# Batch 0's block means of v by products with its own tiles, and the dense layer's first chunk in two runs of pieces

## The chip, the cores and the metric

One core of a Trainium2 chip runs the kernel; the other cores are idle. The metric is the device time of one execution in microseconds; lower is better. The engines are named as in the profile: PE (TensorE) multiplies, PEld is its weight load, DVE (VectorE), ACT (ScalarE) and POOL (GpSimd) work on elements, and SP (SyncE) here only issues DMAs, in the order in which they stand in its program.

## What is computed

```python
# attention: q, k, v are (2, 8, 768, 64); window 16, block 32
k_sum = k.reshape(B, H, nb, block, D).max(axis=3)
v_sum = v.reshape(B, H, nb, block, D).mean(axis=3)      # the block means of v
scores_l = where(|i - j| < 16, scale * q @ k.T, -1e9)
scores_s = scale * q @ k_sum.T + log(block)
a = softmax(concat([scores_l, scores_s]))
x = (a @ concat([v, v_sum])).reshape(1536, 512)
...
# dense layer, 512 -> 2048 -> 512
h = x @ w_in
g = where(h > 0, h, exp(min(h, 0)) - 1)
x = g @ w_out
...
# router and experts: top 1 of 8 by cosine, then relu(x @ w1[e]) @ w2[e] times the gate
```

The weights of the dense layer arrive as 64-bit floats (the kernel reads them as pairs of 32-bit words).

## The kernel before

**Attention.** Each batch has 8 heads, taken as 4 pairs. A pair has 12 query tiles of 64 tokens, in 3 groups of four, so a batch has 12 groups, numbered `sc0` to `sc11` and so on. For a pair the tile `vw` holds, for each query tile, 96 rows of v around it (loaded by `load_v`, `vw<-in_v_dram`, two loads of the middle and four of the ends) and in rows 96 to 119 the 24 block means. `kw` holds keys and block maxima (`ks`) alike, `qbd` the queries. A group runs scores (`sc`, PE), mask with row minimum (`pt`, `mn`, DVE, L395), exp (ACT, L400), sums' reciprocal (DVE), scaling (POOL, L413), transposes (`tp`, PE), their copy (`pT`), products with `vw` (`pv`, PE), and a split of the result into a high and a low part (`xT`, ACT L448 and DVE L456).

The block means come from a second load of v: `load_vst` (L205) brings four heads with a block to each partition, as 96 rows of 32 x 64. `v_summary` sums the first four heads on DVE (four reductions, L213), `v_summary_pool` the other four on POOL (nine additions, L227); `load_vsum` sends the mean tile `vm` by DMA into rows 96 to 119 of `vw`, repeated for the 12 query tiles.

**Dense layer.** The 768 tokens of a batch are two chunks of 384. The 2048 hidden columns are 16 pieces of 128. A step is one piece for one chunk, 64 steps in all: batch 0 chunk 0 with pieces 0 to 15, then chunk 1, then batch 1's chunks. A piece's weights are loaded as pairs of words (`rw`, `rv`), scaled on ACT or POOL (L156, L154) and put together by three DVE operations for each half (L170, L172, L176, `cv` and `vt`); both chunks and both batches use the result `vt`. In each step they are split into a high part (ACT, L186) and a low part (DVE or POOL, L190), both in `wt`. Then come twelve `hp` products (L557 to L559), ELU on ACT and DVE (`e`, `gt`, L564 to L581), and nine `y` products (L596 to L598) that add up over a chunk's 16 steps in three PSUM banks. `y_out` copies these (ACT, L605) and stores them.

**Order.** A string, `ORDER`, lists the program by hand as atoms: `sc3` is the scores of group 3, `b4.00` a conversion of piece 4, `up5` the `hp` products of step 5, `dn5` its `y` products, a letter after a colon the engine. In before it covers batch 0's attention and the steps up to 11 (`G0 = 12`). From there a loop writes each step, and batch 1's attention is put between steps 12 and 37 by `at_step` and `attn_slots`. Each engine runs its share in that order; waits are on tiles and buffers. SP issues a load only when the eighth load before it is in.

Of the kernel before, what the change touches and what calls it, by code (L numbers as in the profile page):

```python
# [41 lines left out]
C_N = C_SLOT + NSLOT  # L42
# [9 lines left out]
lk00:l lk01 c0 lk10:s lk11 lk20:l lq00 lq01 lq20 c1 lt0 ox1 kt00 kt01 mq0 mq1 km00:v km01:v ks0 ke01:a ke00:v  # L52
mk0 kt11 qt00 qo001:a qo000:a qt01 qo011:a qo010:a le01 lk21 lq21 kt10 km10:a lq30 lk30:l le00 kw0:p km11:v
ox0 sc0 sc2 ks1 ex0 ex2 vs00 sc1 ke10:v ex1 kw1:a rt0 no0:p mk1 lq10 ke11:p rt2 no2:p kt20 lq11 qt10 qt11
qo110:a lk31 lv00 lq31 vs01 vs02 qo101:v qo100:v qo111:a vs03 rt1 no1:p kt31 qt20 kt21 km20:a km21:a tr0 sc3
lt1 lv01 le11 td0:a ls01 ls00 ke20:v ex3 ks2 kw2:a vs10 vs11 vs12 ke21:p tr2 sc4 ex4 qo200:v sc5 qt30 lv10
# [25 lines left out]
def fused_kernel(ctx, tc, q, k, v, w_in, w_out, emb, tau, w1, w2, consts, toks, minit, out):  # L82
# [137 lines left out]
    def v_summary_pool(b, r, n0, n1):  # L220
# [7 lines left out]
        if n1 == 10:  # L228
            vsum[b, r] = vm = at.tile([4 * NBLK, D], F32, tag="vm", name="vm", bufs=3)
# [4 lines left out]
    QK = {}  # L234
# [229 lines left out]
    def attn_slots(b):  # L464

        NG, LAG = 3 * NPAIR, 3
        normed = [0]

        def drain(d):

            if d < 2:
                a_out(b, NG - 5 + d)
            if d < 3:
                a_tr(b, NG - 3 + d)
                a_turned(b, NG - 3 + d)
                a_pv(b, NG - 4 + d)
            if d == 2:
                a_out(b, NG - 3)
            if d == 3:
                a_out(b, NG - 2)  # L480
                a_pv(b, NG - 1)
            if d == 4:
                a_out(b, NG - 1)

        def slot(s):
            p, r = s // 3 + 1, s % 3
            prep = s < NG and p < NPAIR
            if s >= NG:
                drain(s - NG)
                return  # L490
            if prep and r == 0 and s:
                prep_k(b, p)
                prep_k_out(b, p)
            if 0 <= s - LAG - 2 < NG:
                a_out_hi(b, s - LAG - 2)
            if s < NG:
                a_scores(b, s)
                a_exp(b, s)
            if s == 0:
                prep_k(b, p)  # L500
                prep_k_out(b, p)
            if s == 1:
                prep_ks(b, p)
            if prep and r:
                prep_q(b, p, r - 1)
            if prep and r == 1:
                prep_w(b, p)
            while normed[0] < (s - 1 if s < NG - 3 else s if s < NG - 1 else NG):
                a_root(b, normed[0])
                a_norm(b, normed[0])  # L510
                normed[0] += 1
            if prep and r:
                prep_q_out(b, p, r - 1)
            if 0 <= s - LAG - 2 < NG:
                a_out_lo(b, s - LAG - 2)
            if 0 <= s - LAG < NG:
                a_tr(b, s - LAG)
                a_turned(b, s - LAG)
            if prep and r == 0 and s:
                prep_ks(b, p)  # L520
            if 0 <= s - LAG - 1 < NG:
                a_pv(b, s - LAG - 1)
            if prep and r == 0 and p + 2 < NPAIR:
                load_k(b, p + 2)
            if prep and r == 2 and p + 2 < NPAIR:
                load_q(b, p + 2)
# [774 lines left out]
```

## Time and profile before

| | us |
|---|---|
| runs of the kernel, median of 3 | 562.68 (561.32 to 563.0) |
| the profiled execution, its own time | 561.42 |
| its span in the trace | 559.6 |
| PE, DVE, ACT, POOL busy | 517.4, 425.7, 354.0, 270.7 |
| first dense step starts | 55.76 |
| step 32 (batch 1) starts | 229.67 |

The span is the time from the first to the last instruction of one execution; the own time holds also what lies around it. Busy time counts an engine's instructions as the profiler saw them; an engine's idle time costs something only where the others wait for it. PE's matmul records come two to a product where the operands are 32-bit floats, so counts in the trace are larger than in the program.

### The profile page before, as it was taken

How to read it: one execution, taken by the hardware profiler on the slowest of the kernel's cores; microseconds unless marked ns; L12 is line 12 of the kernel's file. 1: busy time of each engine (PE TensorE's matmuls, PEld its weight loads, DVE VectorE, ACT ScalarE, POOL GpSimd, SP SyncE). 2: the span in 40 equal slices, each digit the busy share in tenths (PEclk: the TensorE clock that was granted, in tenths of full speed). 3: DMA queues.
4: the chain of work that ended last, by engine and by line, in shares of the span. 5: the costliest groups of instructions: out<-in, count | busy, mean ns of one | idle time of the engine just before them, and what ended most of it. 6: DMA issues, size and time to landing. Idle time of an engine off the chain costs nothing.

```text
span 559.6 us, 10282 instructions
## 1 busy us (share of the span) xinstructions
PE 517.4 (92%) x3270; PEld 455.2 (81%) x3270; DVE 425.7 (76%) x1053; ACT 354.0 (63%) x870; POOL 270.7 (48%) x274
## 2 busy tenths in 40 slices
PE   4986898999899999998999999999999999999991
PEld 4765786879788898896888998889779989999980
DVE  4999999988997665488776488866899777656671
ACT  3888685666767675565476655665565586566570
POOL 1477686876385332344457546765376532121010
PEclk9999998999999999999999999999999999999997
DMA  8999865669302014020100223718946399965000
GB/s 216 205 262 218 301 216 201 177 168 218 108 1 53 20 35 169 20 77 19 37 2 2 75 57 95 249 54 281 340 163 208 111 339 316 335 215 181 20 29 14
DMA packets 98939, 81.28 MB, mean 145 GB/s; under 512 B 38159, under 2 KB 83599, under 8 KB 98368
## 3 DMA queue, kind: packets, MB, share of 16 engines
q1 hardware_dynamic: 96256, 73.72, 44.7%
q0 software_dynamic: 2624, 6.84, 3.4%
q8 instruction: 28, 0.46, 0.4%
q14 instruction: 31, 0.25, 0.2%
HBM read 73.03 MB, written 6.94 MB: 143 GB/s over the span
## 4 chain that ended last, share of the span: by engine, by line
PE 31%; issue 8%; DVE 7%; ACT 5%; POOL 3%; POOLq 0%; ACTq 0%; DVEq 0%
PE shp L891 3%; PE o L914 3%; PE shp L892 3%; PE shp L890 3%; PE o L915 3%; PE o L913 3%; DVE ydj L640 3%; POOL wt L190 2%; DVE e L573 2%; PE y L598 1%; ACT wt L186 1%; DVE wt L190 1%; PE y L596 1%; PE y L597 1%; ACT gt L577 1%
## 5 line engine op out<-in xcount | busy, mean ns | idle before, releaser
L581 POOL TENSOR_TENSOR gt<-e,gt 128x384 fp32r<-128x384 f32 x63 | 64.0, 1016 | 87.7 <-ACT gt L577 50.1
L190 POOL TENSOR_TENSOR wt<-vt,wt 128x512 fp32r<-128x512 f32 x60 | 79.5, 1333 | 39.4 <-ACT wt L186 35.1
L190 DVE TENSOR_TENSOR wt<-mv,wt 128x512 fp32r<-128x512 f32 x113 | 80.6, 750 | 15.3 <-ACT wt L186 8.2
L557 PE MATMUL hp<-xT,wt 128*128 128x384 f32 x256 | 86.8, 339 | 3.8 <-DVE vt L176 2.7
L186 ACT ACTIVATE wt<-vt 128x512 fp32r<-128x512 f32 x128 | 75.5, 626 | 21.9 <-PE y L598 11.9
L559 PE MATMUL hp<-xT,wt 128*128 128x384 f32 x256 | 86.8, 339 | 0.2
L558 PE MATMUL hp<-xT,wt 128*128 128x384 f32 x256 | 86.3, 337 | 0.6 <-DVE xT L456 0.6
L598 PE MATMUL y<-wt,gt 128*128 128x512 f32 x192 | 77.9, 406 | 3.0 <-POOL gt L581 2.0
L596 PE MATMUL y<-wt,gt 128*128 128x512 f32 x192 | 78.7, 410 | 1.8 <-ACT gt L577 1.8
L190 DVE TENSOR_TENSOR wt<-vt,wt 128x512 fp32r<-128x512 f32 x68 | 57.7, 861 | 29.4 <-ACT wt L186 29.2
L577 ACT ACTIVATE gt<-e 128x384 fp32r<-128x384 f32 x64 | 33.5, 524 | 71.2 <-DVE e L573 67.3
L597 PE MATMUL y<-wt,gt 128*128 128x512 f32 x192 | 76.3, 398 | 0.0
L186 ACT ACTIVATE wt<-mv 128x512 fp32r<-128x512 f32 x128 | 73.8, 629 | 0.0
L640 DVE SCALAR_TENSOR_TENSOR ydj<-yp,en_b 128x512 bf16<-128x512 f32 x72 | 46.4, 686 | 12.6 <-ACT yp L636 5.9
L890 PE MATMUL shp<-sx,wt 128*128 128x256 f32 x192 | 54.4, 283 | 1.0 <-DVE ydj L640 0.7
L891 PE MATMUL shp<-sx,wt 128*128 128x256 f32 x192 | 54.2, 282 | 0.3 <-DVE sx L845 0.3
L557 PEld LDWEIGHTS hp<-xT,wt 128*128 128x128 f32 x256 | 48.4, 189 | 7.4 <-issue 2.4
L892 PE MATMUL shp<-sx,wt 128*128 128x256 f32 x192 | 54.0, 281 | 0.0
L558 PEld LDWEIGHTS hp<-xT,wt 128*128 128x128 f32 x256 | 48.5, 189 | 3.5 <-DVE xT L456 0.9
L598 PEld LDWEIGHTS y<-wt,gt 128*128 128x128 f32 x192 | 36.5, 190 | 16.1 <-POOL gt L581 6.9
L559 PEld LDWEIGHTS hp<-xT,wt 128*128 128x128 f32 x256 | 48.3, 189 | 1.0 <-POOL wt L190 1.0
L400 ACT ACTIVATE pt<-pt,mn 128x120 f32<-128x120 f32 x96 | 36.6, 384 | 13.9 <-DVE mn L395 13.2
(175 smaller groups left out, 1194.6 us busy)
## 6 DMA issues: line engine op xcount, KB each, us to landing
mv<-in_moe_w_dram SPq DMA_DIRECT2D x128, 256.0 KB
rw<-in_moe_w_in_dram SPq DMA_DIRECT2D x16, 512.0 KB
rv<-in_moe_w_out_dram SPq DMA_DIRECT2D x13, 512.0 KB
vw<-in_v_dram SPq DMA_DIRECT2D x16, 240.0 KB
kn<-in_k_dram SPq DMA_DIRECT2D x16, 192.0 KB
qn<-in_q_dram SPq DMA_DIRECT2D x16, 192.0 KB
vst<-in_v_dram SPq DMA_DIRECT2D x4, 768.0 KB
y_d<-ysb SPq DMA_DIRECT2D x12, 256.0 KB
```

The costliest lines, as they stand in the source:

```text
L186: nc.scalar.activation(out=wt[:, 0, :], in_=src, func=AF.Copy)
L190: eng.tensor_tensor(out=wt[:, 1, :], in0=src, in1=wt[:, 0, :].bitcast(F32), op=ALU.subtract)
L557: nc.tensor.matmul(hp, wh, xt[:, 0, kk, :], start=(kk == 0), stop=False)
L558: nc.tensor.matmul(hp, wh, xt[:, 1, kk, :], start=False, stop=False)
L559: nc.tensor.matmul(hp, wl, xt[:, 0, kk, :], start=False, stop=(kk == KD - 1))
L581: eng.tensor_tensor(out=gt[:, 1, :], in0=self.e, in1=gt[:, 0, :].bitcast(F32), op=ALU.subtract)
L596: nc.tensor.matmul(yp, gh, woh, start=(f == 0), stop=False)
L597: nc.tensor.matmul(yp, gh, wol, start=False, stop=False)
L598: nc.tensor.matmul(yp, gl, woh, start=False, stop=(f == KF - 1))
L890: nc.tensor.matmul(hp, wh, x[:, 0, kk, :], start=(kk == 0), stop=False)
L891: nc.tensor.matmul(hp, wh, x[:, 1, kk, :], start=False, stop=False)
L892: nc.tensor.matmul(hp, wl, x[:, 0, kk, :], start=False, stop=(kk == KD - 1))
```

## The change

Three things change together.

First, batch 0's block means. A new constant, two columns `C_BLK` of 96 rows, holds 1/32 for the two blocks that lie in the middle of a query tile's 96 rows. For a pair, `v_blocks` multiplies each of the 12 tiles of `vw` (as weights, 96 x 128) with these two columns into 24 columns of one bank; `v_blocks_out` copies them to `vT`, `v_blocks_turn` turns them with one product against the identity, and `v_blocks_spread` copies the 24 x 128 result to rows 96 to 119 of `vw`, repeated 12 times. Their atoms are `vp`, `vo`, `vt` and `vx`, with the number of the pair. Batch 0's two `load_vst`, its sums and its eight `load_vsum` go; batch 1 keeps them.

Second, the order of the dense steps: `RUNS`. Chunk 0 of batch 0 meets pieces 0 to 5, chunk 1 meets all sixteen, then chunk 0 meets 6 to 15. Chunk 0's half sum leaves PSUM through a DRAM tile `y_h` (`y_part`: an ACT copy and a store for each of three tiles) and comes back (`y_back`) to be added in `y_out`. The router's part of chunk 1 now stands ahead of that of chunk 0.

Third, the string `ORDER` is new and reaches to step 32 (`G0 = 33`): batch 1's attention stands in it, as atoms in capital letters, in place of `attn_slots`.

```diff
+HC = 6
...
+    def v_blocks(b, p):
+
+        QP[b, p, "v"] = vb = bank("vb")
+        for i in range(NQ):
+            nc.tensor.matmul(
+                vb[:, 2 * i:2 * i + 2], vw[p % 2][0:WIN, i, :], cst[0:WIN, C_BLK:C_BLK + 2], start=True, stop=True
+            )
+
+    def v_blocks_out(b, p, eng):
+        vb = QP[b, p, "v"]
+        QP[b, p, "v"] = vT = at.tile([P, NBLK], F32, tag="vT", name="vT", bufs=2)
+        copy(vT, vb[:, 0:NBLK], eng)
+
+    def v_blocks_turn(b, p):
+        vT = QP[b, p, "v"]
+        QP[b, p, "v"] = vr = bank("vr")
+        nc.tensor.matmul(vr[WIN:NK, 0:P], vT, ident, start=True, stop=True)
+
+    def v_blocks_spread(b, p, eng):
+        vr = QP.pop((b, p, "v"))
+        copy(vw[p % 2][WIN:NK, :, :], vr[WIN:NK, 0:P].unsqueeze(1).to_broadcast([NBLK, NQ, P]), eng)
...
-            if f == KF - 1:
-                for t in range(NTT):
-                    y_out(b, c, t)
+                nc.tensor.matmul(yp, gl, woh, start=False, stop=self.last)
...
+    def y_part(b, c, t):
+
+        ysb = small([P, DM], "ysb")
+        nc.scalar.activation(out=ysb, in_=Y[b, c][t], func=AF.Copy)
+        nc.sync.dma_start(out=y_h[t], in_=ysb)
+
+    def y_back(t):
+        YPART[t] = yh = small([P, DM], "yh")
+        nc.sync.dma_start(out=yh, in_=y_h[t])
+
     def y_out(b, c, t):
         ysb = small([P, DM], "ysb")
-        nc.scalar.activation(out=ysb, in_=Y[b, c][t], func=AF.Copy)
+        if (b, c) == (0, 0):
+            nc.vector.tensor_tensor(out=ysb, in0=Y[b, c][t], in1=YPART.pop(t), op=ALU.add)
+        else:
+            nc.scalar.activation(out=ysb, in_=Y[b, c][t], func=AF.Copy)
...
-    G0 = 12
+    G0 = 33
...
-    steps = [Dense(b, c, f) for b in range(B) for c in range(NCH) for f in range(KF)]
+    RUNS = ((0, 0, 0, HC), (0, 1, 0, KF), (0, 0, HC, KF)) + tuple((1, c, 0, KF) for c in range(NCH))
+    steps = [Dense(b, c, f, f == lo, f == hi - 1) for b, c, lo, hi in RUNS for f in range(lo, hi)]
...
-        g0 = tails([(0, 0), (0, 1)], T0, lambda g: 4 if g < 41 else 3)
+        g0 = tails([(0, 1), (0, 0)], T0, lambda g: 4 if g < 41 else 3)
...
+    for g in range(2):
+        c[16 + 32 * g:48 + 32 * g, C_BLK + g] = 1.0 / 32
```

The line numbers of the changed kernel differ: `sc` is L428 there, `tp` L464, `pv` L482, `hp` L533 to L535, `ka` L355 and L360, `qp` L386. In the rows below a number behind `x` counts equal instructions of the program in a row.

**The start of PE.** In the kernel before, PE's program begins so (`ka` turns and `qp` are the keys and queries being transposed):

```order
L310 MATMUL ka<-cst,kn 64x128 x12
L315 MATMUL ka<-cst,kn 128x128 x2
L341 MATMUL qp<-cst,qn 128x128 x6
L315 MATMUL ka<-cst,kn 128x128 x4
L383 MATMUL sc<-kw_110,qbd_108 128x120 x12
L310 MATMUL ka<-cst,kn 64x128 x8
L341 MATMUL qp<-cst,qn 128x128 x6
L310 MATMUL ka<-cst,kn 64x128 x4
```

In the changed kernel it begins so; `vb` are the products with the two columns, `vr` the turn of their result:

```order
L386 MATMUL qp<-cst,qn 128x128 x6
L355 MATMUL ka<-cst,kn 64x128 x12
L360 MATMUL ka<-cst,kn 128x128 x6
L386 MATMUL qp<-cst,qn 128x128 x6
L428 MATMUL sc<-kw_113,qbd_111 128x120 x4
L263 MATMUL vb<-cst,vw_115 128x2 x12
L428 MATMUL sc<-kw_113,qbd_111 128x120 x8
L428 MATMUL sc<-kw_114,qbd_112 128x120 x12
L275 MATMUL vr<-cst,vT 24x128
```

The first twelve `vb` products stand inside the scores of pair 0, behind its group that needs only four of them, and ahead of the other five groups of pairs 0 and 1.

**The first loads.** SP's queue in the kernel before, from its fifth load on:

```order
L249 DMA kn<-in_k_dram 128x3x128
L261 DMA qn<-in_q_dram 128x3x128 x3
L1027 DMA cst<-in_consts_dram 128x634
L205 DMA vst<-in_v_dram 96x2048
L280 DMA vw_112<-in_v_dram 80x64
L281 DMA vw_112<-in_v_dram 80x64
L249 DMA kn<-in_k_dram 128x3x128
L261 DMA qn<-in_q_dram 128x3x128 x2
L249 DMA kn<-in_k_dram 128x3x128
L280 DMA vw_112<-in_v_dram 80x64
L281 DMA vw_112<-in_v_dram 80x64
```

And in the changed kernel; `vw_115` is the tile of pair 0, which all its twelve `vb` products read, and `vw_116` that of pair 1:

```order
L325 DMA vw_115<-in_v_dram 80x64
L326 DMA vw_115<-in_v_dram 80x64
L306 DMA qn<-in_q_dram 128x3x128
L320 DMA vw_115<-in_v_dram 96x10x64
L306 DMA qn<-in_q_dram 128x3x128 x2
L1017 DMA cst<-in_consts_dram 128x636
L320 DMA vw_116<-in_v_dram 96x10x64
L306 DMA qn<-in_q_dram 128x3x128
L325 DMA vw_115<-in_v_dram 80x64
L326 DMA vw_115<-in_v_dram 80x64
L294 DMA kn<-in_k_dram 128x3x128
L320 DMA vw_115<-in_v_dram 96x10x64
```

The loads of `vst` are gone, and the last of pair 0's v loads is the nineteenth load of all.

**DVE in the middle of the dense steps.** In the kernel before, from the ELU (`e<-e,hp`) of step 8 to that of step 9, with the three conversion operations of each half (`cv`, `cv`, `vt`) between:

```order
L573 SCALAR_TENSOR_TENSOR e<-e,hp 128x384
L566 TENSOR_SCALAR e<-hp 128x384
L170 TENSOR_SCALAR cv<-rv 128x512
L172 SCALAR_TENSOR_TENSOR cv<-rv,cv 128x512
L176 SCALAR_TENSOR_TENSOR vt<-rv,cv 128x512
L170 TENSOR_SCALAR cv<-rw 128x512
L172 SCALAR_TENSOR_TENSOR cv<-rw,cv 128x512
L176 SCALAR_TENSOR_TENSOR vt<-rw,cv 128x512
L573 SCALAR_TENSOR_TENSOR e<-e,hp 128x384
```

And in the changed kernel, from the ELU of step 12 to that of step 13:

```order
L549 SCALAR_TENSOR_TENSOR e<-e,hp 128x384
L195 TENSOR_SCALAR cv<-rw 128x512
L197 SCALAR_TENSOR_TENSOR cv<-rw,cv 128x512
L201 SCALAR_TENSOR_TENSOR vt<-rw,cv 128x512
L542 TENSOR_SCALAR e<-hp 128x384
L238 TENSOR_REDUCE vm<-vst 96x16
L549 SCALAR_TENSOR_TENSOR e<-e,hp 128x384
```

In before two halves are converted there in one step, in the changed kernel one half, and the first sum of batch 1's block means stands beside it.

## Rows read from the trace of the kernel before

**Rows 1.** The page, section 1: busy us (share of the span) xinstructions.

```profile
PE 517.4 (92%) x3270; PEld 455.2 (81%) x3270; DVE 425.7 (76%) x1053; ACT 354.0 (63%) x870; POOL 270.7 (48%) x274
```

**Rows 2.** Windows: length, busy of PE PEld DVE ACT POOL, clock, DMA, GB/s.

```profile
0.00:55.76 55.76, 39.31 (x439) 33.31 (x439) 45.04 (x174) 38.83 (x144) 28.22 (x47) 0.97 0.95 225
...
129.64:168.61 38.97, 36.62 (x243) 33.13 (x242) 35.41 (x96) 26.97 (x85) 23.33 (x29) 1.00 0.39 99
168.61:229.67 61.06, 60.60 (x467) 53.97 (x466) 39.35 (x125) 38.81 (x113) 20.48 (x22) 1.00 0.22 64
229.67:377.50 147.83, 144.44 (x721) 126.26 (x720) 109.14 (x272) 93.84 (x203) 83.08 (x76) 0.99 0.21 65
```

**Rows 3.** Windows, steps 0 to 16 in one; columns as above.

```profile
55.76:129.64 73.88, 68.42 (x330) 59.18 (x331) 70.11 (x115) 50.74 (x104) 57.08 (x54) 0.98 0.69 212
```

**Rows 4.** Timeline of PE, one attention step: start us, us, line, tile, count.

```profile
189.47 0.33 PE L557 MATMUL hp<-xT,wt 128*128 128x384 f32 x1
...
191.57 1.05 PE L383 MATMUL sc<-kw,qbd 128*128 128x120 f32 x8
192.46 0.60 PE L419 MATMUL tp<-cst,pt 128*120 128x128 f32 x4
192.99 0.69 PE L437 MATMUL pv<-pT,vw 120*64 120x64 f32 x16
193.60 0.50 PE L596 MATMUL y<-wt,gt 128*128 128x512 f32 x1
...
195.78 0.33 PE L557 MATMUL hp<-xT,wt 128*128 128x384 f32 x1
```

**Rows 5.** The page, section 6: DMA issues, their count and KB each.

```profile
vw<-in_v_dram SPq DMA_DIRECT2D x16, 240.0 KB
kn<-in_k_dram SPq DMA_DIRECT2D x16, 192.0 KB
...
vst<-in_v_dram SPq DMA_DIRECT2D x4, 768.0 KB
...
vw<-vm SPq DMA_DIRECT2D x16, 72.0 KB
vw<-in_v_dram SPq DMA_DIRECT2D x32, 20.0 KB
cst<-in_consts_dram SPq DMA_DIRECT2D x1, 317.0 KB
```

**Rows 6.** Windows of lines L213, L227, L400: busy, count, clock, DMA, GB/s.

```profile
0.00:55.76 55.76, 4.04 (x4) 0.97 0.95 225
...
0.00:55.76 55.76, 6.10 (x9) 0.97 0.95 225
...
0.00:55.76 55.76, 19.27 (x96) 0.97 0.95 225
```

**Rows 7.** Timeline of PE near 318 us; line L383: ns min/median/max.

```profile
318.23 0.29 PE L736 MATMUL rp<-ohb,ones 128*128 128x8 bf16 x6
318.38 0.48 PE L596 MATMUL y<-wt,gt 128*128 128x512 f32 x1
...
L383 PEld LDWEIGHTS sc<-kw,qbd x192: 186/192/337, 12.4 to 204.9; 128*128 128x128 f32 x192
```

**Rows 8.** Timeline of the first 16 us.

```profile
4.94 2.83 PE L310 MATMUL ka<-cst,kn 128*64 128x128 f32 x24 [4.94 <-DMA cst<-in_consts_dram]
...
10.06 0.62 SPq L249 DMA_DIRECT2D kn<-in_k_dram  x1
...
15.05 0.33 SPq L281 DMA_DIRECT2D vw<-in_v_dram  x1
```

**Rows 9.** Lines by form: busy us, mean ns of one, idle before.

```profile
L845 DVE TENSOR_TENSOR sx<-stp,sx 128x512 fp32r<-128x512 f32 x14 | 9.6, 689 | 11.8 <-ACT sx L844 11.8
L605 ACT ACTIVATE ysb<-y 128x512 f32<-128x512 f32 x12 | 6.7, 593 | 4.1 <-PE y L598 3.7
...
L448 ACT ACTIVATE xT<-pv 128x256 fp32r<-128x256 f32 x16 | 5.9, 373 | 0.6 <-PE pv L437 0.6
```

More of the change, by code (lines that the diff above doesn't have):

```diff
@@ L51 @@
 ORDER = """
[L52 to L56, printed above, removed]
@@ L77 @@
-z14.0:a z13.0:a b13.00 b13.01 b13.02 gh10 gl10:v
+lk10:s lk00:l lk01 lk11 lq00 c0 ox1 mq0 mk0 le00 ox0 mq1 lq10 lv00 lq01 lq11 c1 lv10 qt00 qo001:a qt10 qo000:a
+qo101:v lq20 le01 lk30:l qo100:v lv01 lv11 lq30 lk20:l kt00 km00:v lw0.0 lw0.1 kt01 lw1.0 kt10 lw1.1 kt11 qt01 km11:v
+rl km01:v ks0 km10:a qo011:a qt11 qo010:a ks1 ke01:a ke00:a qo110:a kw0:p ke10:v kw1:a qo111:a mk1 lk21 ke11:p sc2
+le11 vp0 vo0:v sc0 le10 sc1 ex2 lk31 ex0 lq21 sc3 lq31 sc5 sc4 lw2.0 ex1 z0.0:p vt0 rt2 rt0 no2:p ex3 qt20 no0:p
@@ L78 @@
+TD10:a OH9 ea29:v gl28:p up30 TD11:a OL9 dh29 eb29 uh32 ec29 dl29:v PV10 gh29 ea30:v PV11 OH10 gl29:v eb30 dn28 OL10
+OH11 OL11 dh30 ul31:v late ec30 up31 dl30:v gh30 uh33 ul32:v gl30:p dn29 dh31 ea31:v eb31 ul33:p dl31:v up32 ec31
+uh34 gh31 ul34:v gl31:p dn30
 """
@@ L121, in fused_kernel @@
     y_d = [dr_p.tile([S, DM], F32, name=f"y_d{b}") for b in range(B)]
+    y_h = [dr_p.tile([P, DM], F32, name=f"y_h{t}") for t in range(NTT)]
     en_d = dr_p.tile([NE, DM], F32, name="en_d")
@@ L210, in v_summary @@
         if n == 0:
-            vsum[b, r] = at.tile([4 * NBLK, D], F32, tag="vm", name="vm", bufs=3)
+            vsum[b, r] = at.tile([4 * NBLK, D], F32, tag="vm", name="vm", bufs=2)
         vm, w = vsum[b, r], D // parts
@@ L228, in v_summary_pool @@
         if n1 == 10:
-            vsum[b, r] = vm = at.tile([4 * NBLK, D], F32, tag="vm", name="vm", bufs=3)
+            vsum[b, r] = vm = at.tile([4 * NBLK, D], F32, tag="vm", name="vm", bufs=2)
             nc.gpsimd.tensor_tensor(
@@ L462, in a_out @@
         a_out_lo(b, n)
[L464 to L526, printed above, removed]
-            if r == LAG % 3 and 2 <= (s - LAG) // 3 + 1 < NPAIR:
-                load_v(b, (s - LAG) // 3 + 1)
-                load_vsum(b, (s - LAG) // 3 + 1)
-        return [lambda s=s: slot(s) for s in range(NG + 5)]
     RT = {}
@@ L538, in fused_kernel, with __init__ @@
     class Dense:
-        def __init__(self, b, c, f):
-            self.b, self.c, self.f = b, c, f
+        def __init__(self, b, c, f, first, last):
+            self.b, self.c, self.f, self.first, self.last = b, c, f, first, last
             self.neg = (b, c) == (0, 0) or b == 1
@@ L589, in down @@
             b, c, f, gt, wt = self.b, self.c, self.f, self.g, self.d
-            if f == 0:
+            if self.first:
                 Y[b, c] = [bank(f"y{t}") for t in range(NTT)]
@@ L1064, in fused_kernel @@
                 atom(f"b{f}.{n}{o}", conv_bits, f, (n, o))
+    for f in range(G0 + 2):
         for key, fn in (
@@ L1070, in fused_kernel @@
             atom(f"{key}{f}", fn, f)
+        for t in range(NTT):
+            atom(f"yp{f}{t}", lambda f=f, t=t: y_part(steps[f].b, steps[f].c, t))
+            atom(f"yo{f}{t}", lambda f=f, t=t: y_out(steps[f].b, steps[f].c, t))
+    for t in range(NTT):
+        atom(f"yb{t}", y_back, t)
     atom("rl", route_loads)
@@ L1074, in fused_kernel @@
     atom("rb", route_consts_b)
-    atom("lt2", load_vst, 1, 0)
+    atom("late", open_late)
+    atom("yl", y_load, 0, 1, 0)
     with tc.manual_schedule():
@@ L1204, in fused_kernel @@
                 steps[g - 2].down()
+                if g - 2 < GD and steps[g - 2].last:
+                    for t in range(NTT):
+                        y_out(steps[g - 2].b, steps[g - 2].c, t)
             for fn in extra.get((g, True), []):
```

176 lines of the change are left out of this document (87 added, 89 removed).

## Prediction

> **What bounds the kernel now.** I read the page's busy shares first [rows 1]: PE is busy 517.4 of 559.6 us, DVE 425.7, ACT 354.0. PE is the engine whose idle time costs, but a mean hides the stages, so the windows came next [rows 2]. Their cuts are the starts of dense steps 0, 16, 22 and 32 (the steps between 0 and 16 in a window of their own [rows 3]). In the head (0 to 55.76) PE is busy 39.31 us, DVE 45.04, ACT 38.83, and the DMA engines 0.95 of the time: nothing is full but the loads, and the stage ends on a chain through all of them. In steps 0 to 16 (55.76 to 129.64) DVE is busy 70.11 of 73.88 us [rows 3]; it converts the weights. From step 22 on PE is busy 60.60 of 61.06.
>
> An undisturbed dense step takes PE 4.17 us: twelve `hp` at 0.174 (189.47 to 191.57) and nine `y` at 0.232 (193.60 to 195.78) [rows 4]. The same row group gives an attention group: 0.89 for `sc` (8 records, 0.111 each, two to a product), 0.53 for `tp`, 0.61 for `pv`. The program counts 12 such groups, 24 `qp` (0.11 each) and about 2.6 us of `ka` in batch 1: 12 x 2.03 + 2.6 + 2.6 = 29.6. So steps 0 to 32, 55.76 to 229.67, took 173.9 us, of which 32 x 4.17 + 29.6 = 163.0 is PE's own work and **10.9 us are stalls** (each step counted whole, though the last `y` stand behind the cut, in both kernels alike). By the same count, with batch 1's groups where the order has them: 73.88 - 16 x 4.17 - 1.2 = 6.0 in steps 0 to 16; 3.2 of 38.97 in 16 to 22, 8%; 1.7 of 61.06 in 22 to 32, 2.8%.
>
> **The head, term by term.** Removed are two loads of 768 KB and eight of 72 KB, 2.1 MB [rows 5]; DVE's four sums, 4.04 us; POOL's nine adds, 6.10 us [rows 6]. Neither engine is full there (DVE 45.04 of 55.76, POOL 28.22), so this time does not come off the end by itself; the loads do, where PE waits for one.
>
> Added on PE are 48 products with two moving columns. They are fp32, so two records each: 96. The trace has no such product. Bounds: 25 ns (128 weight columns, 8 moving ones, but bf16: six from 318.23 to 318.38) and 192 ns (the median of an fp32 weight load of 128 columns when its end is taken as it stands) [rows 7]. Nearest is `sc`, fp32, 128 weight columns, 111 ns; but 120 columns move there, so 111 may be the moving and not the load. I take 111, as fp32 weights are what these products share with it: 96 x 0.111 = 10.7 us. The ends give 2.4 and 18.4.
>
> The Trainium skill ("TensorE: Matmul & The Clock Gate", section "LDWEIGHTS (loading the stationary operand)") speaks against the change here: a load's time goes by its weight columns, not its rows, about 107 ns for 128 of them, and two moving columns hide none of it; by it the products cost 10.2 us. No row of before separates this from the moving.
>
> PE's work ahead of the first step, at these prices: `sc` 12 x 0.89 = 10.7; `tp` 12 x 0.53 = 6.4; `pv` 10 x 0.61 = 6.1 (two of the twelve now stand behind step 0); `qp` 24 x 0.11 = 2.6; `ka` 7.9 (78 records at 0.102: the 24 at 4.94 take 2.83 us with the tail of the last [rows 8]); products 10.7; `vr` 0.9. Sum 45.3, where before has 45.3 - 10.7 - 0.9 + 1.2 = 34.9.
>
> When can it start? In the new order the first products stand behind only 5.4 us of PE work, ahead of `sc0`, and wait for the whole first `vw` tile, the 19th load. In before SP issues a load when the eighth before it is in: at 10.06 with 1.64 MB landed, at 15.05 with 2.75 [rows 8] (bytes summed over SP's queue from [rows 5]; `qn` is as large as `kn`), 0.22 MB/us. The new order has 3.18 MB up to its 19th load: 15.05 + 0.43/0.22 = 17.0; taken as 16.5 to 17. All of PE queues behind this wait, and DVE's masks behind the copy `vo0` of its result. So step 0 starts no earlier than 16.8 + 45.3 - 5.4 = 56.7.
>
> One more wait is visible in the order: the first `pv` needs `td0`, which stands on ACT behind six groups of exps (the head's 96 records take ACT 19.27 us [rows 6], so 1.6 for a group's eight) and the first spread copy `vx` (by 256 columns 0.373 and 512 columns 0.593, 1536 come to 1.47 [rows 9]). From a first exp at 19.8 that is 19.8 + 9.6 + 1.5 = 30.9 less what overlaps, about 30.4; PE has by then done 16.8 + 11.2 = 28.0. That is 2.4 us. **Step 0 at about 59.1, 3.3 later than 55.76.** What would let it come earlier is a cheaper product.
>
> **Steps 0 to 32.** PE gains the two `pv` groups, 1.2 us. Chunk 0's half sums go out and come back: three ACT copies (0.593 each [rows 9]), three stores and three loads of 256 KB, three adds on DVE in place of copies (0.689 each [rows 9]). ACT is busy 50.74 of 73.88 there [rows 3]: hidden; without that cover they cost 1.8 us. On SP's queue the three returns stand ahead of batch 1's loads and the last weight pieces; the DMA engines were busy 0.69 of that time and 0.39 in the next stage, so these come late for nobody. DVE's 2.1 us come at step 22 and count in its sum.
>
> The main term is the stalls. Conversion of sixteen pieces now stretches over 22 steps, since ten of the pieces are first met by chunk 1 later and chunk 0's ten come after. Counted in the new order with before's durations, DVE against PE is 47.1 : 51.2 in steps 0 to 12, 48.7 : 49.9 in 12 to 22 and 52.8 : 63.4 in 22 to 32; in before it was 70.1 : 67.9 in steps 0 to 16. DVE is no longer over PE anywhere, but within 3% of it in steps 12 to 22. What a stage loses then, from the rows: 22 to 32 lost 2.8% with DVE at 39.35 of 61.06; 16 to 22 lost 8% with DVE at 35.41 of 38.97 [rows 2]; and DVE as the bound was kept 95% busy [rows 3], so 95.8 us of it need at least 100.9, just PE's 101.1. I take 2.8% where DVE has room (51.2 and 63.4: 3.2) and 5%, between the two rows, in the tie (2.5): **5.7 us of stalls instead of 10.9**.
>
> **Sum.** +3.3 +1.2 -5.2 = -0.7 against the profiled execution, whose own time is 561.42: 560.7. After step 32 the code is the same with the two chunks' tails exchanged; nothing is costed there, covered by PE at 144.44 of 147.83 us. The median of the runs, 562.68, lies 1.3 above the profiled execution, so I give **561.0**.
>
> **Rivals.**
> - *Cheap products* (25 to 55 ns). For it: nothing but two columns move, and six bf16 ones took 25. Against: those are not fp32. PE's head shrinks by 5 to 8 us, but ACT then sets the end: of its work ahead of step 0, 40.6 us counted in the new order (exps 19.3, four `vx` 5.9, the rest copies at the rates of [rows 9]), about 5.5 lie before its first exp, which comes at 17.5; step 0 is then at about 53. With the same stalls -2.7 + 1.2 - 5.2 = -6.7: about 554.5.
> - *The tie costs what 16 to 22 cost* (slower). In steps 0 to 22 DVE's `e` and `vt`, POOL's `gt` and ACT stand in each other's way at 8% as in steps 16 to 22 [rows 2], DVE being as full: 101.1 x 0.08 + 1.8 = 9.9 us of stalls. +3.3 + 1.2 - 1.0 = +3.5: about 565. It decides once the stage loses over 6.5%. The attention of batch 1 now lies within steps 20 to 31 and chunk 0's conversions before it, which is why I hold the lower value likelier.
> - *Full price of a load* (192 ns): +7.8 us in the head, about 568.5. Against it: `sc`'s loads have the same 192 and yet follow at 111.
> - *The new order holds stalls at 2.8% throughout*: 164.5 x 0.028 = 4.6, a gain of 1.1 more, 559.6; part of the likeliest case's range.
>
> **How the numbers follow.** A difference under 0.3% (1.7 us) can't be told from none in this kernel. The sum with its stalls between 4 and 8 us: 0.45, of which 0.17 under -1.7, 0.21 within, 0.07 above; own range 558 to 564. Cheap products, or a load that lets PE start sooner: 0.25, all faster. The tie at 8% or more: 0.20, all but 0.02 slower. Full price of a load: 0.08, slower. Something that no row shows: 0.02 slower. Faster 0.42, within 0.23, slower 0.35. The range takes in most of the cheap products and of the tie: 552 to 567.
>
> **What would show it.** Step 0's first `hp`: near 59 (near 53: cheap products; over 62: dear ones). The product's cadence, twelve program products as 24 records: 2.7 us at my price. PE idle until 16.5 to 17 before the first of them. Step 32 at about 229 (229.67 - 0.7), with DVE over 95% busy in steps 12 to 22 and PE losing some 2.5 us there. If steps 0 to 16 still take 74 us, the main term is wrong; if step 32 comes by 223, the head is.

## The result, and the profile after

The changed kernel takes 569.6 us (median of 4 runs, 569.42 to 571.32) against 562.62 (561.32 to 563.0): a ratio of 1.0135, with a 95% interval of 1.011 to 1.016. It is slower by some 7 us (6.98 between the medians, 7.6 by the ratio), and the forecast was 561.0. The profiled execution took 569.42 with a span of 567.6.

Of the page: the busy shares that answer to [rows 1], and the row of the granted clock (the share of 2.4 GHz that PE was given, in tenths) in 40 slices of 14.2 us; behind it the same row of the kernel before, in slices of 14.0 us.

```profile
PE 533.6 (94%) x3374; PEld 474.8 (84%) x3374; DVE 422.9 (75%) x1058; ACT 361.5 (64%) x872; POOL 265.4 (47%) x263
PEclk9698599999999999999999999999999999999996
...
PEclk9999998999999999999999999999999999999997
```

PE is busier than before, and the clock row has a 6, an 8 and a 5 within its first five slices, where the kernel before had only nines. The windows that answer to [rows 2] and [rows 3]: head, steps 0 to 16, steps 16 to 32, all of 0 to 32, the rest, and the tie of steps 12 to 22.

```profile
0.00:74.04 74.04, 60.31 (x510) 54.85 (x510) 40.48 (x172) 42.93 (x145) 22.54 (x40) 0.79 0.62 165
74.04:139.73 65.69, 65.23 (x354) 58.18 (x351) 63.20 (x107) 52.24 (x104) 55.37 (x47) 1.00 0.70 204
139.73:236.61 96.88, 96.88 (x722) 87.40 (x720) 81.78 (x233) 70.32 (x207) 45.88 (x50) 1.00 0.36 100
```

```profile
74.04:236.61 162.57, 162.11 (x1075) 145.59 (x1071) 144.98 (x339) 122.56 (x310) 101.25 (x97) 1.00 0.50 142
236.61:567.60 330.99, 311.21 (x1795) 274.37 (x1793) 237.48 (x549) 196.03 (x419) 141.63 (x126) 0.99 0.42 137
122.99:173.12 50.13, 50.13 (x276) 45.48 (x275) 48.41 (x98) 34.33 (x80) 34.22 (x37) 1.00 0.64 160
```

Two changes of opposite sign stand there. The head is 18.3 us longer: the first `hp` comes at 74.04 instead of 55.76. Steps 0 to 32 are 11.3 us shorter, 162.57 instead of 173.9: 65.69 against 73.88 in steps 0 to 16 and 96.88 against 100.0 in 16 to 32. The rest takes 330.99 where it took 329.9. Together +18.3 - 11.3 + 1.1 = +8.1; the span went from 559.6 to 567.6, the same but for rounding.

The head's row also shows a granted clock of 0.79 (0.97 before). Half of 2.4 GHz is the lower level, 1.2 GHz, so 0.79 stands for 74.04 x 0.21 x 2 = 31 us at half clock, in which 74.04 x 0.21 = **15.5 us of PE's work are lost** (55.76 x 0.03 = 1.7 before). PE idles 74.04 - 60.31 = 13.7 us, and 60.31 - 15.5 = 44.8 us is its work at full clock.

PE's timeline in the head, and windows of one microsecond around it with the granted clock (the number behind the count).

```profile
15.60 1.72 PE L428 MATMUL sc<-kw,qbd 128*128 128x120 f32 x8 [2.12 <-POOL kw L344]
17.11 5.13 PE L263 MATMUL vb<-cst,vw 96*128 96x2 f32 x24
22.10 6.67 PE L428 MATMUL sc<-kw,qbd 128*128 128x120 f32 x40
...
34.65 0.69 PE L482 MATMUL pv<-pT,vw 120*64 120x64 f32 x16 [1.84 <-ACT pT L470]
...
36.20 2.74 PE L263 MATMUL vb<-cst,vw 96*128 96x2 f32 x24
38.87 0.69 PE L482 MATMUL pv<-pT,vw 120*64 120x64 f32 x16
...
48.71 6.32 PE L428 MATMUL sc<-kw,qbd 128*128 128x120 f32 x40 [1.99 <-DVE qbd L402]
54.87 3.22 PE L263 MATMUL vb<-cst,vw 96*128 96x2 f32 x24
57.94 2.04 PE L428 MATMUL sc<-kw,qbd 128*128 128x120 f32 x8
...
60.63 5.12 PE L263 MATMUL vb<-cst,vw 96*128 96x2 f32 x24
65.68 0.62 PE L275 MATMUL vr<-cst,vT 128*24 128x128 f32 x2
66.23 1.96 PE L464 MATMUL tp<-cst,pt 128*120 128x128 f32 x8
```

```profile
15.00:16.00 1.00, 0.40 (x3) 1.00 1.34 175
16.00:17.00 1.00, 1.00 (x7) 0.50 1.31 189
25.00:26.00 1.00, 1.00 (x6) 0.50 0.15 33
27.00:28.00 1.00, 1.00 (x11) 1.00 0.85 253
...
57.00:58.00 1.00, 1.00 (x7) 0.50 0.96 384
68.00:69.00 1.00, 1.00 (x5) 0.50 0.00 0
71.00:72.00 1.00, 1.00 (x21) 1.00 0.00 0
```

Four stretches ran at half clock: about 16.0 to 26.2, 39.9 to 43.3, 50.1 to 53.5 and 57.0 to 70.6. The first begins after PE had waited 2.1 us for `kw` (the row at 15.60 follows that wait), and the 24 records of pair 0's products lie wholly in it: 22.10 - 17.11 = 5.0 us, about 0.21 each. Pair 1's products ran at full clock, 38.87 - 36.20 = 2.7 us, 0.111 each, and the clock fell a microsecond behind them. The third begins behind the wait of 1.99 us for `qbd`. The last stretch begins 2 us behind the first record of pair 2's products (54.87) and holds pair 3's, 65.68 - 60.63 = 5.05 us, and all that follows them up to 70.6. In the kernel before there was one such stretch, 3.4 us from 12.3, behind a wait of 2.59 us for `kw`.

### The profile page after: what moved, and what is told of

Read it like the earlier page. It is cut to its first block, busy times and chain, and to the rows that moved or that the text cites. A ratio compares the mean times of both kernels' runs of the same rounds, so it can differ in the third digit from the quotient of the medians.

```text
span 567.6 us, 10488 instructions
## 1 busy us (share of the span) xinstructions
PE 533.6 (94%) x3374; PEld 474.8 (84%) x3374; DVE 422.9 (75%) x1058; ACT 361.5 (64%) x872; POOL 265.4 (47%) x263
## 3 DMA queue, kind: packets, MB, share of 16 engines
q1 hardware_dynamic: 94496, 73.13, 43.3%
## 4 chain that ended last, share of the span: by engine, by line
PE 66%; DVE 11%; issue 8%; ACT 8%; POOL 3%; DMA 1%; SPq 1%; POOLq 0%; ACTq 0%; DVEq 0%
PE sc L428 5%; PE y L574 5%; PE y L572 5%; PE y L573 5%; PE hp L535 5%; PE hp L533 5%; DVE ydj L628 5%; PE hp L534 5%; PE shp L879 3%; PE o L902 3%; PE shp L880 3%; PE shp L878 3%; PE o L903 3%; PE o L901 3%; PE vb L263 3%
## 5 line engine op out<-in xcount | busy, mean ns | idle before, releaser
L215 POOL TENSOR_TENSOR wt<-vt,wt 128x512 fp32r<-128x512 f32 x62 | 81.5, 1321 | 42.1 <-ACT wt L211 37.5
L533 PE MATMUL hp<-xT,wt 128*128 128x384 f32 x256 | 87.3, 341 | 0.0
L535 PE MATMUL hp<-xT,wt 128*128 128x384 f32 x256 | 86.3, 337 | 0.3 <-POOL wt L215 0.3
L572 PE MATMUL y<-wt,gt 128*128 128x512 f32 x192 | 77.0, 401 | 3.5 <-ACT gt L553 3.5
L574 PE MATMUL y<-wt,gt 128*128 128x512 f32 x192 | 76.8, 400 | 1.5 <-POOL gt L557 1.5
L573 PE MATMUL y<-wt,gt 128*128 128x512 f32 x192 | 75.7, 394 | 0.0
L215 DVE TENSOR_TENSOR wt<-vt,wt 128x512 fp32r<-128x512 f32 x66 | 60.6, 926 | 17.4 <-ACT wt L211 17.3
L533 PEld LDWEIGHTS hp<-xT,wt 128*128 128x128 f32 x256 | 48.1, 188 | 2.3
L535 PEld LDWEIGHTS hp<-xT,wt 128*128 128x128 f32 x256 | 48.0, 188 | 0.9 <-POOL wt L215 0.9
L445 ACT ACTIVATE pt<-pt,mn 128x120 f32<-128x120 f32 x96 | 36.6, 382 | 17.3 <-DVE mn L440 17.0
```

Of the source, the lines that this page charges most:

```text
L215: eng.tensor_tensor(out=wt[:, 1, :], in0=src, in1=wt[:, 0, :].bitcast(F32), op=ALU.subtract)
L533: nc.tensor.matmul(hp, wh, xt[:, 0, kk, :], start=(kk == 0), stop=False)
L535: nc.tensor.matmul(hp, wl, xt[:, 0, kk, :], start=False, stop=(kk == KD - 1))
L572: nc.tensor.matmul(yp, gh, woh, start=self.first, stop=False)
L573: nc.tensor.matmul(yp, gh, wol, start=False, stop=False)
L574: nc.tensor.matmul(yp, gl, woh, start=False, stop=self.last)
```

## The experiments

The two questions were whether the products' two columns take the clock down, or PE's waits in the new order do (theory A and rival B of the expectations), and what each part of the change is worth. A loss by the clock is worked out as above, from one window over the head: its length times one minus the granted clock. Where PE idles at half clock this counts too much, most of all in e3_second_load. Each ratio is taken against executions of the kernel before that ran beside that kernel, so it is not the quotient of the medians shown here. Heads, clocks and steps are those of one profiled execution each.

| kernel | total, median us | ratio, 95% interval | first `hp` | clock in the head, loss us | PE idle in the head | steps 0 to 32 |
|---|---|---|---|---|---|---|
| before | 562.62 | | 55.76 | 0.97, 1.7 | 16.5 | 173.9 |
| changed | 569.6 | 1.0135 (1.011 to 1.016) | 74.04 | 0.79, 15.5 | 13.7 | 162.6 |
| e1_wide | 561.77 | 0.9983 (0.9963 to 1.0004) | 67.40 | 0.95, 3.4 | 17.5 | 162.5 |
| e2_v_moves | 562.05 | 0.9997 (0.997 to 1.0024) | 64.81 | 0.95, 3.2 | 16.4 | 162.6 |
| e3_second_load | 571.13 | 1.0152 (1.0121 to 1.0182) | 77.62 | 0.78, 17.1 | 31.9 | 162.4 |
| e6_one_product | 627.81 | | 61.98 | 0.89, 6.8 | 19.4 | 162.5 |
| e12_wide_later | 567.07 | 1.0064 (1.0038 to 1.009) | 72.25 | 0.88, 8.7 | 18.1 | 162.4 |
| e10_part_one | 569.83 | 1.015 (1.011 to 1.0191) | 65.04 | 0.87, 8.5 | 9.5 | 171.5 |
| e11_part_one_wide | 569.03 | 1.0133 (1.0096 to 1.017) | 61.77 | 0.97, 1.9 | 12.4 | 172.9 |
| e7_old_head | 552.67 | 0.9838 (0.9817 to 0.986) | 55.31 | 0.97, 1.7 | 16.3 | 164.5 |

**Wide products.** The one edit is the width of what moves; 126 columns of ones stand behind the two block columns in the constant, and each product overwrites the surplus of the one ahead of it.

```diff
-                vb[:, 2 * i:2 * i + 2], vw[p % 2][0:WIN, i, :], cst[0:WIN, C_BLK:C_BLK + 2], start=True, stop=True
+                vb[:, 2 * i:2 * i + P], vw[p % 2][0:WIN, i, :], cst[0:WIN, C_BLK:C_BLK + P], start=True, stop=True
...
```

> The changed kernel with one edit: each of the 48 products moves 128 columns instead of two (the two block columns and 126 columns of ones beside them, whose results the next product overwrites). Theory A, two moving columns leave the array nearly idle, so the clock falls to 1.2 GHz after the products and stays there while they run: of the 29.5 us at half clock in the head only the short falls after waits stay (about 6.5 us), so some 11.5 us come back; first hp near 62.5, total near 558. A product's record still takes 0.11 us, since the load of 128 weight columns sets it at either width. Rival B, the clock falls because of PE's waits and the new order, whatever the products move: first hp at 74, total 569 to 570. Rival C, the moving costs time of its own: a record takes over 0.13 us and the head gets longer by 2 us or more.

Measured: 561.77. The head's window and two groups of products.

```profile
0.00:67.40 67.40, 49.88 (x510) 44.65 (x510) 39.60 (x172) 42.50 (x145) 22.20 (x40) 0.95 0.66 175
```

```profile
34.16 0.97 PE L482 MATMUL pv<-pT,vw 120*64 120x64 f32 x16 [2.75 <-ACT pT L470]
...
49.69 4.70 PE L428 MATMUL sc<-kw,qbd 128*128 128x120 f32 x40 [2.63 <-DVE qbd L402]
54.23 2.85 PE L263 MATMUL vb<-cst,vw 96*128 96x128 f32 x24
56.91 1.05 PE L428 MATMUL sc<-kw,qbd 128*128 128x120 f32 x8
```

Twelve products take 56.91 - 54.23 = 2.7 us with 128 columns, as they took with two at full clock (2.7 at 36.20), so rival C falls. The clock is 0.95 instead of 0.79: 12 us of lost work came back, from nothing but more columns. The first fall, behind the wait for `kw`, is still there, but lasts from 17.3 to 20.7 and not for 10.2 us; one more stands at 34.4 to 37.8, behind the wait for `pT`. That is theory A. The size was missed: the first `hp` came at 67.4, 6.6 us earlier and not 11.5. PE's busy time fell by 10.4 us (60.31 to 49.88), but it idles 17.5 us instead of 13.7: the first `pv` waits 2.75 us for ACT's `pT` (1.84 in the changed kernel), the scores of pair 2 wait 2.63 for DVE's `qbd` (1.99). That ACT and DVE set this head once the clock holds is read from these waits and was not shown by a run of its own.

**v moves.** The sides exchanged: 24 constant columns are the weights, the 128 columns of the v tile move, and the sum over twelve products is already turned.

```diff
-        QP[b, p, "v"] = vb = bank("vb")
+        QP[b, p, "v"] = vr = bank("vr")
         for i in range(NQ):
+            o = C_BLK + NBLK - 2 - 2 * i
             nc.tensor.matmul(
-                vb[:, 2 * i:2 * i + 2], vw[p % 2][0:WIN, i, :], cst[0:WIN, C_BLK:C_BLK + 2], start=True, stop=True
+                vr[WIN:NK, 0:P], cst[0:WIN, o:o + NBLK], vw[p % 2][0:WIN, i, :], start=(i == 0), stop=(i == NQ - 1)
             )
...
```

> The changed kernel with the sides of the products exchanged: 24 columns of a constant are the weights (two of them not zero), a tile of v moves with its 128 columns, twelve products add up to the 24 means of a pair as rows, so the copy vT and the turn are gone. Theory A: as with the wide products the clock holds, and the chain is shorter by a copy and a turn for each pair: first hp 60 to 62, total 556 to 558. Rival B (PE's waits and the order): the clock falls all the same, first hp at 72 to 74, total 567 to 570.

Measured: 562.05, first `hp` at 64.81, some 3 us behind the forecast, with PE idle for 16.4 us; the clock holds as in e1_wide (0.95).

```profile
52.21 2.80 PE L263 MATMUL vr<-vw,cst 96*24 96x128 f32 x24
54.94 1.15 PE L428 MATMUL sc<-kw,qbd 128*128 128x120 f32 x8
```

The records cost as much with 24 weight columns: 54.94 - 52.21 = 2.73 us. So a record takes 0.11 us with 24 weight columns and 128 moving (here), with 128 and 2 (0.111 at 36.20) and with 128 and 128 (e1_wide): either side of 128 columns takes that long, and both together no longer.

**A probe in the kernel before**, where PE waits for nothing: two blocks of 48 products ahead of steps 45 and 52.

```diff
+            n = {(1, 0, 13): 2, (1, 1, 4): P}.get((self.b, self.c, self.f), 0)
+            one = cst[:, C_ONE:C_ONE + P]
+            for _ in range(48 if n else 0):
+                nc.tensor.matmul(hp[:, 0:n], one, one[:, 0:n], start=True, stop=True)
```

> The kernel before with products added whose results are overwritten: 48 (96 records) with two moving columns ahead of step 45's hp, and 48 with 128 moving columns ahead of step 52's, both with a tile of ones as fp32 weights, in stretches where PE waits for nothing. Theory A: the clock is 1.0 around both; it falls to half during or behind the narrow ones and stays at 1.0 through the wide ones; at full clock a record takes 0.11 us at either width. Rival B (only waits bring it down): 1.0 through both, each stretch 10.7 us. If the records are cheaper at two columns than at 128, the weights are not what sets their time.

PE's timeline at both blocks, and windows of the clock.

```profile
291.12 16.38 PE L558 MATMUL hp<-cst 128*128 128x2 f32 x96
307.35 0.67 PE L561 MATMUL hp<-xT,wt 128*128 128x384 f32 x1
```

```profile
339.50 10.88 PE L558 MATMUL hp<-cst 128*128 128x128 f32 x96
...
350.13 0.42 PE L561 MATMUL hp<-xT,wt 128*128 128x384 f32 x1
```

```profile
287.00:291.00 4.00, 4.00 (x22) 1.00 0.00 0
291.00:295.00 4.00, 4.00 (x38) 1.00 0.00 0
295.00:299.00 4.00, 4.00 (x23) 0.58 0.01 2
303.00:307.00 4.00, 4.00 (x21) 0.50 0.00 0
307.00:311.00 4.00, 4.00 (x14) 0.50 0.00 0
311.00:315.00 4.00, 4.00 (x17) 0.79 0.00 0
339.00:343.00 4.00, 4.00 (x35) 1.00 0.00 0
347.00:350.00 3.00, 3.00 (x30) 1.00 0.02 5
```

Without any wait, and with PE busy in every window, the clock is 1.0 for the first 4 us of the narrow products, then 0.5 until some 5 us behind them; through the wide ones it is 1.0. Narrow: 16.2 us; wide: 350.13 - 339.50 = 10.6 us, 0.111 a record. At full clock the narrow ones cost the same: 36 of the 38 records in 291 to 295 are theirs (the others are `y`), begun within 295 - 291.12 = 3.9 us, some 0.11 each. This is theory A by itself, in one execution: a PE that the profile calls busy did not hold the clock up. (The run took 589.67 us in all.)

The Trainium skill ("TensorE: Matmul & The Clock Gate", section "LDWEIGHTS (loading the stationary operand)") gives a load's time by its weight columns alone, columns / 1.2 ns; an estimate by it is 107 ns for 128 columns. The trace agrees at full clock (about 0.11 us a record). At half clock the record takes about 0.21. The same page of the Trainium skill (section "HAM oscillation — how this bites in real kernels") names PE's idle gaps as what brings the clock down. The falls behind waits go that way, but the probe's rows do not: there the clock falls without a gap, and the measurement decides.

**One product for a pair.**

```diff
-        for i in range(NQ):
-            nc.tensor.matmul(
-                vb[:, 2 * i:2 * i + 2], vw[p % 2][0:WIN, i, :], cst[0:WIN, C_BLK:C_BLK + 2], start=True, stop=True
-            )
+        nc.tensor.matmul(vb[:, 0:NBLK], vw[p % 2][0:WIN, 0, :], cst[0:WIN, C_ID:C_ID + NBLK], start=True, stop=True)
```

> The changed kernel with one product for a pair in place of twelve (24 columns of the identity move), so the block means are not computed; everything else stays. Theory A: the 88 records that are left out take 9.8 us of PE at full clock and about 11.5 us of half clock with them: first hp near 53, total near 549. Rival B (clock falls with waits, whatever the products do): only the products' own time goes, at the mixed clock they ran at about 15 us: first hp near 60, total 555 to 560.

Without the means the router gets other values, and the stages behind step 32 do other work (400.9 us; 3590 PE records in all where the changed kernel has 3374), so the total doesn't count. The first `hp` came at 61.98, nearer to rival B's 60 than to theory A's 53, and the clock does not hold.

```profile
0.00:61.98 61.98, 42.54 (x422) 36.91 (x423) 41.55 (x172) 42.73 (x145) 22.45 (x40) 0.89 0.74 197
```

With 8 records left of the 96 the new head still loses up to 6.8 us to the clock, and PE idles 19.4 us. So the two-column products explain the larger part of the loss but not all of it, and even with almost none of them the new head ends 6.2 us later than the old one. My theory A had no term for that. Along these runs the 18.3 us split into 6.2 (55.76 to 61.98: the new head almost without products), 5.4 (to 67.40: products of 128 columns) and 6.6 (to 74.04: two columns instead). The first two are not cleanly apart, since this run loses more to the clock than e1_wide.

**The second load in the new order.** The `vp`, `vo`, `vt` and `vx` atoms are taken out; `lt`, `vs` and `ls` put in:

```diff
+ c1 lt0 ... ks1 vs00 vs01 vs02 vs03 ... lq31 lt1 ls00 ls01 ... no3:p vs10 vs11 ... no5:p vs12 vs13 vs14
+ td1:a ls10 ls11 ... td3:a vs15 vs16 vs17 vs18 vs19 ... no7:p ls20 ls21 ... tr6 ls30 ls31
```

> The new order of pieces and atoms, but batch 0's means made as before: two loads of 768 KB, DVE's and POOL's sums, eight loads into vw; no products. Theory A (the products are the loss): PE has 11.6 us less to do in the head and the clock falls only after waits; first hp 54 to 59, steps 0 to 32 in about 163 us as in the changed kernel, total 549 to 555. Rival B (the new order itself makes PE wait and the clock fall): first hp over 66, total over 561. The second loads put 2.1 MB ahead of the weights, which may cost up to 5 us of that.

```profile
43.17 1.60 PE L481 MATMUL pv<-pT,vw 120*64 120x64 f32 x15 [9.07 <-DMA vw<-vm]
```

By the signs set down ahead of it rival B came out (first `hp` at 77.62). But the first `pv` waits 9.07 us for a mean's DMA, and the clock is at half from 28 to 48.5: where I put these atoms, they make a wait of their own. So 571.13 says nothing on the products and much on the placing; the experiment is inconclusive for what it was made for. Steps 0 to 32 again took 162.4.

**Pair 0's products later.**

```diff
-le11 vp0 vo0:v sc0 le10 sc1 ex2 lk31 ex0 lq21 sc3 lq31 sc5 sc4
+le11 sc0 le10 sc1 ex2 lk31 ex0 lq21 sc3 lq31 sc5 sc4 vp0 vo0:v
```

> As e1_wide, but pair 0's products and the copy behind them (vp0, vo0) stand behind the scores of the first six groups instead of ahead of five of them. If the exps on ACT are the chain after the start (in e1_wide the first exp comes at 22.7, since DVE's first mask stands behind the copy of the products' result): first exp near 19, first pv some 3 us earlier, first hp 64 to 65.5, total 558 to 560. Rival, the chain goes over the products themselves (spread copy, then pv): the first pv and the first hp (67.4) stay, total 561 to 563.

Measured: 567.07, in ten runs between 562.38 and 567.3. The first exp did come at 18.55, but the first `pv` at 35.36 and the first `hp` at 72.25.

```profile
0.00:72.25 72.25, 54.11 (x511) 48.46 (x511) 39.38 (x172) 43.06 (x145) 22.12 (x40) 0.88 0.64 164
```

Both theories missed: PE now has four short waits between 26 and 36 (for DVE's `vT`, twice POOL's `pt`, ACT's `pT`; two in e1_wide), and half clock rose from 6.8 to 17 us. The spread of the runs goes with the clock: the two shortest (562.38 and 562.8) had 0.986 over the whole run, the six longest 0.976 or 0.977. Which waits bring it down stays open: ahead of pair 2's scores PE waits 2.63 us for `qbd` here and in e1_wide alike, and the clock fell at 51.1 here and not there.

**Part one alone, in the old order.** The second load and its atoms go; the products stand behind each pair's v loads.

```diff
+ le11 vp0 vo0:v ... sc4 vt0 vx0:a ... lv11 vp1 vo1:v ... tr3 vt1 vx1:a
+ lv20 vp2 vo2:v ... sc11 vt2 vx2:a ... le31 vp3 vo3:v ... uh1 vt3 vx3:a
```

Two first runs had `vp3` behind `lv30`, ahead of the last end rows, and computed one head's means from old rows:

> The kernel before, in its order, with the first part of the change alone: batch 0's means by the 48 two-column products in place of the second load, each pair's first product behind the last of its v loads. Theory A (two-column products let the clock fall): half clock in the head rises from 3.4 us to over 13 us, and with 11.6 us of new PE work, part of it in PE's 20 us of waits, the first hp comes at 64 to 72; steps 0 to 32 stay at 174; total 571 to 580. Rival B (the fall belongs to the new order): half clock stays at 3 to 7 us, first hp at 56 to 63, total 562 to 570.

> The same kernel as e4_part_one but each product moves 128 columns, the last 126 of them ones whose results are overwritten. Theory A: the record still takes 0.11 us and half clock goes back to 3 to 7 us, so the first hp comes 4 to 10 us before that of e4_part_one. Rival B: no difference between the two.

They took 568.98 and 566.71 us, with the first `hp` at 66.16 and 63.99, and 9.9 and 5.1 us lost to the clock (twice that at half clock). The two-column kernel has the half clock of theory A, but a shorter total; the wide one came only 2.2 us earlier and kept more half clock than forecast. With the order mended:

> As e4_part_one (the order before, means by two-column products), but pair 3's products now stand behind all of that pair's v loads; in e4_part_one and e9_part_one_wide they stood ahead of its last end rows, so those two runs computed one head's means from stale rows. Theory A: first hp 64 to 69, half clock in the head over 13 us, steps 0 to 32 in 172 to 175, total 567 to 573: part one alone costs the old order 5 to 11 us.

> As e9_part_one_wide (128 columns move) with the same mending. Theory A: a record still takes 0.11 us, half clock in the head 3 to 10 us, first hp 2 to 6 us before that of e10_part_one, total 563 to 568. Rival B: no difference between the two.

```profile
0.00:65.04 65.04, 55.51 (x542) 48.68 (x543) 43.67 (x178) 44.36 (x147) 22.60 (x37) 0.87 0.68 195
65.04:236.50 171.46, 163.80 (x1040) 145.25 (x1039) 142.53 (x330) 117.31 (x303) 100.44 (x101) 1.00 0.42 123
```

```profile
0.00:61.77 61.77, 49.36 (x542) 43.92 (x542) 43.34 (x176) 43.60 (x146) 22.25 (x37) 0.97 0.71 198
61.77:234.66 172.89, 165.28 (x1042) 146.58 (x1039) 143.31 (x331) 117.41 (x305) 98.40 (x101) 0.99 0.43 125
```

Two columns: 569.83, the head 9.3 us longer, 8.5 us lost to the clock (0.87). 128 columns: the clock is that of before (0.97), the head still 6.0 us longer. So exchanging the second load for the products' 10.7 us of work costs this head 6 us, PE's waits (12.4 us instead of 16.5) hiding a part, and the clock 3.3 more. Both heads and both half clocks (17 and 4 us) lie in their forecasts; e10_part_one's steps (171.5) and e11_part_one_wide's total lie up to a microsecond outside. In the totals the two differ by only 0.8 us, within their spread (567.4 to 572.1): the mechanism is seen in the heads, and what it is worth in the old order is not settled to better than 0 to 3 us.

**The old head and the new steps.** The string of the kernel before up to `up0`, that of the changed kernel from there on, without the atoms that were already done; `z4.0`, `dl0`, `rl`, `rc` and `rb` stand behind steps 1 to 11.

```diff
-ORDER = (atoms of the changed kernel ahead of up0) up0 ...
+ORDER = (atoms of the kernel before ahead of up0) up0 ... z4.1:a up1 z4.0:a dl0:p ea0:a ...
```

> The changed kernel with the string of the kernel before up to the first dense step (second load, sums on DVE and POOL, no products) and the new string from there on, so chunk 0 meets six pieces and batch 1's attention stands where the new order has it. If head and steps are worth what each kernel shows: first hp at 55.8, steps 0 to 32 in 162.5 to 165, the rest 331, so a span of 549 to 552 and a total of 551 to 554, a ratio near 0.98. Rival: the steps are short in the changed kernel only because its late head had already converted and loaded more of the weights; then steps 0 to 32 take 168 to 174 and the total is 557 to 562.

```profile
0.00:55.31 55.31, 39.01 (x438) 33.49 (x438) 44.24 (x174) 38.79 (x144) 28.10 (x47) 0.97 0.95 228
55.31:219.76 164.45, 161.94 (x1038) 145.98 (x1039) 142.57 (x339) 120.16 (x304) 102.06 (x101) 0.99 0.53 152
219.76:550.60 330.84, 311.36 (x1795) 274.33 (x1793) 237.75 (x549) 196.02 (x419) 141.39 (x126) 0.99 0.43 137
```

552.67 us, as the sum of both halves said: 55.3 + 164.5 + 330.8. The rival falls: the steps took 164.45 us, not 168 to 174, without the late head. A part did come with that head: with two `pv` groups less to do (1.2 us of PE) these steps take 1.9 us longer than the changed kernel's, so some 3 us of those short steps are that head's. This kernel beats both others: 0.9838 of the kernel before, interval 0.9817 to 0.986.

## Why the prediction was wrong

**The head, "Step 0 at about 59.1".** It came at 74.04, 14.9 us later, and two steps of that sum failed.

The first is the price of the work: all of it was taken at full clock. Every duration came from a kernel whose head runs at 0.97, and a record's 0.111 us was carried over to an instruction that moves 2 columns where `sc` moves 120. At full clock that price was right (0.111 at 36.20), and so was the amount of work (45.3 us against 44.8). But the head ran at 0.79 and lost 15.5 us. With 128 columns 3.4 of these stay, so some 12 us belong to the two columns, with 6.6 us of the first `hp` (74.04 against 67.40). No rival had it: the dear rival priced the products at 192 ns for another reason, and its 568.5 was near the result by accident. That the two columns are the cause is shown by e1_wide, by the pair e10_part_one and e11_part_one_wide, and by the probe. That the clock also falls in the new head without them is shown by e6_one_product and e12_wide_later; which waits do it stays open.

The second is the waits. 59.1 - 45.3 = 13.8 us of idle against 13.7 looks right and is luck. The sum has 11.4 us ahead of the products and 2.4 behind; the trace has 9.0 (three waits, 6.75 + 0.17 + 2.12) and 4.7, and with the clock held (e1_wide) 10.2 and 7.3. Nothing stood in the sum for the wait of pair 2's scores for DVE's `qbd` (1.99 us; 2.63 in e1_wide). And the chain on ACT was about as long as summed (11.3 us from the first exp to `td0`, against 11.1) but began late: the first exp came at 22.70, in e1_wide too, not at 19.8, since DVE's first mask stands behind the copy of the first products' result.

```profile
22.70 0.40 ACT L445 ACTIVATE pt<-pt,mn 128x120 f32<-128x120 f32 x1 [6.23 <-DVE mn L440]
...
34.00 1.09 ACT L470 ACTIVATE pT<-tp 120x512 f32<-120x512 f32 x2
```

So the first `pv` came at 34.65, and at 34.16 in e1_wide, not at 30.4.

**"What would let it come earlier is a cheaper product".** Not so simply: with the clock held, PE's idle time rose to 17.5 us. The head would have been missed by 8.3 us even without the products' half clock (67.40 against 59.1: 1.2 of work, 3.4 lost to the clock that is left, 3.7 of idle), and e1_wide's 561.77, close to the 561.0 of the forecast, is two errors that cancel: its steps 0 to 32 are 7.4 us shorter than forecast (162.5 against 173.9 + 1.2 - 5.2).

**The load of 2.1 MB, and the wait for the 19th load.** The products started at 17.11, near my 16.5 to 17, but by luck: PE waited for POOL's `kw` until 15.60 and then did the scores, and no wait for the load shows there.

**The stalls, "5.7 us instead of 10.9".** Too high. By the same count, with 51.2 + 49.9 + 63.4 = 164.5 us of work, 162.57 - 164.5 = -1.9, where before had 10.9: a gain of 12.8, not 5.2. A stall below nothing comes from the count of 32 whole steps: only 270 of their 288 `y` products stand between the cuts, in both kernels, so 18 x 0.232 = 4.2 us of work do not belong there, and the stalls are 15.1 us before and 2.3 now. The steps that failed are the shares carried over from the old order. In the tie of steps 12 to 22, priced at 5% or 2.5 us, DVE is busy 48.41 of 50.13 us, as tied as I counted (48.7 : 49.9), and PE does not idle at all: 50.13 - 49.9 = 0.2. In steps 22 to 32, priced at 2.8% or 1.8 us, it is 63.49 - 63.4 = 0.1. The 8% of steps 16 to 22 before belonged to that order. The tie rival falls with it. Whether the split of chunk 0 or the hand order of batch 1's attention brings more was not tried apart; of the 11.3 us, 8.2 lie in steps 0 to 16.

**The last step, "so I give 561.0".** It does not follow: 1.3 us on 560.7 would be 562.0. Nothing above hangs on it.

**The half sums, the router's exchanged tails.** Priced at nothing, and nearly so: the rest of the program took 330.99 against 329.9, and 330.8 in e7_old_head.

## What to carry to other kernels

An instruction that keeps PE busy in the profile need not hold its clock up: price a product with few moving columns at full clock and then at half, for itself and for what stands behind it, and give it more columns, or let the large operand move, where the time is the same as it was here. When two parts of a change act on different stages, a kernel with one half of each order shows in one run what each is worth. And a bound that two engines share cost next to nothing here, in an order without waits in that stage (steps 12 to 22): count the waits, not the ratio.

## What was not expected of the hardware

PE busy in every window and waiting for nothing, its clock still fell from 2.4 to 1.2 GHz within a run of two-column products (1.00 in 291 to 295, 0.58 in 295 to 299), and stayed there for some 5 us of dense `hp` and `y` behind them. A record of a product costs 0.11 us at full clock with 2 or 128 moving columns (128 weight columns), and also with 24 weight columns where 128 columns move; about 0.21 at half clock with two.
